# A spectral block with gated MLP: in stage two, the first gate's product two rounds later, the special column's copies behind the W products, three pairs turned first, the first position zero-padded

## The chip, the cores and the metric

One Trainium2 chip, one of its cores. The metric is the device time of one execution in microseconds, the median of three runs; a profiled execution of the same program gives the rows below.

## What is computed

Two branches on x of 2048 x 512 (float32), each gated by rows that come from a condition vector c:

```python
mod = (_silu(c) @ w_mod).reshape(c.shape[0], 6, 1, -1)
sa, ca, ga, sb, cb, gb = (mod[:, 0], ..., mod[:, 5])
h = _layernorm(x, axis=-1) * (1 + ca) + sa
x = x + ga * _A_ref(h, A_w_r, A_w_i)      # irfft2(rfft2(h) * W), W = w_r + i w_i
h = _layernorm(x, axis=-1) * (1 + cb) + sb
x = x + gb * _B_ref(h, B_w1, B_b1, B_w2)  # dense, Mish, dense
```

## The kernel before

The kernel runs in four stages. Stage one makes the row transform and most of the column transform of the normalised x, in 16 steps. Stage two (about 50 to 98 us) finishes the column transform, multiplies by W and begins the transform back. Stage three (`p3_col`, `p3_row`) finishes the transform back and adds the result, gated, to x. Stage four is the MLP.

Stage two treats the 64 column groups as eight **pairs** p of eight groups each, one pair in a round. A pair passes through five helpers:

- `p2_in(p)`: 16 small transposes on TensorE (L469) into two PSUM banks, then two copies back to `a_sb` by ScalarE (L475; for p = 0 one of them by VectorE, L473). The first bank stays in use, since `p2_shift` reads it.
- `p2_shift(p)`: adds a shift to one position; for p of 2 and more VectorE reads the first bank of `p2_in(p)` for it (L487).
- `p2_mul(p)`: eight matmuls (L494) into a bank of tag A, then one of tag B.
- `p2_prod(p)`: the product with W. VectorE reads bank A (L505, L506), then bank B (L507, L509); GpSimd makes a difference (L508) and a sum (L510; for p = 0, 6 and 7 the sum is on VectorE).
- `p2_out(p)`: 32 matmuls (L521) into two banks of tag C, which ScalarE then copies to `dd` in eight instructions (`store_d`, L395 and L396, in the order first bank, second bank, first, second).

PSUM has four tags, A to D, of two banks each. A bank that is to be filled waits until every reader of the tile that held it is done. Two readers of one bank on different engines are put in program order one behind the other.

A round (the loop at L588) issues, in this order: `p2_mul(p)`; `p2_in(p + 2)`; `p2_prod(p)`; `p2_shift(p + 2)`; a share of the sums for the other modulation rows (`mod_late`: VectorE at L554 to L560, ScalarE at L544, GpSimd at L546, from DMAs of `mod_fetch`); `p2_out(p - 1)`. The order is written out by hand (`manual_schedule`): each engine takes its instructions in just this order, and one that waits holds all that follow on its engine. Pairs 0 and 1 are turned (`p2_in`) ahead of the loop.

The special column (group 0 holds two real columns in one) takes a way of its own: `z_in` in round 0 (its copies: `turned`), `z_mul` in round 1, `z_prod` in round 2, `z_back` in round 4, `z_out` behind the loop. `z_back` transposes twice into a bank of tag D (L446, L447) and then makes `t1` and `t2` from it: `turned(t1, ...)` is a copy by ScalarE (L405), a reversed one by VectorE (L406) and a memset by GpSimd (L407); `t2` gets a memset (L450) and three copies on ScalarE, VectorE, ScalarE (L451 to L453). `reflected` (in `z_mul` and `z_out`) multiplies with these; its second matmul (L411) uses a single column of `t` as weights and writes row 0 alone.

`mod_gate` makes the first gate's row over all partitions: a matmul into a bank of tag D (L564), a copy by ScalarE (L566), and on GpSimd the product into `kiv` (L567), which stage three reads at L707. It stands right behind `z_back` in round 4. `apply_gate` does the like for the second gate at the end of the stage (L571, the same matmul form).

Of the kernel before, what the change touches and what calls it, by code (L numbers as in the profile page):

```python
# [12 lines left out]
P = 128  # L13
# [18 lines left out]
def tile_spectral_block(ctx: ExitStack, tc: tile.TileContext, x_d, w1_d, b1_d, w2_d,  # L32
                        c_d, xt_d, wm_d, wq_d, wz_d, kr_d, km_d, kc_d, ki_d, kf_d, kv_d, kw_d, kp_d, out_d):
    nc = tc.nc
# [33 lines left out]
    def bank(tag):  # L68
        return psum.tile([P, 512], F32, name="bank", tag=tag)

    def buf(tag, dt=F32):
        return work.tile([P, 512], dt, name="buf", tag=tag)
# [96 lines left out]
    st = {}  # L169
# [122 lines left out]
    def shift_sums(lo, hi):  # L292
        ps, pick = st["own"]
        own = modr[:, 2].rearrange("p (e q) -> p e q", e=8)
        nc.vector.tensor_tensor(own[:, :, lo:hi], ps.rearrange("p (e q) -> p e q", e=8)[:, :, lo:hi],
                                pick.unsqueeze(2).to_broadcast([P, 8, hi - lo]), op=ALU.mult)
        nc.vector.tensor_reduce(saz[:, lo:hi], own[:, :, lo:hi].rearrange("p e q -> p q e"),
                                axis=mybir.AxisListType.X, op=ALU.add)
# [105 lines left out]
    def turned(dst, src):  # L404
        nc.scalar.copy(dst[:, 0:P], src)  # L405
        nc.vector.tensor_copy(dst[:, P + 1:2 * P], src[:, P - 1:0:-1])  # L406
        nc.gpsimd.memset(dst[:, P:P + 1], 0.0)  # L407

    def reflected(out, t, w, more=()):
        nc.tensor.matmul(out, t[:, 0:P], w(0), start=True, stop=False)  # L410
        nc.tensor.matmul(out[0:1], t[:, 0:1], w(2), start=False, stop=False)  # L411
        for a, b in more:
            nc.tensor.matmul(out, a, b, start=False, stop=False)
        nc.tensor.matmul(out, t[:, P:2 * P], w(1), start=False, stop=True)

    def z_in():
        z = buf("h")
        turned(z, zs[:, 0])
        st["z", 0] = z

    def z_mul():
        z = st.pop(("z", 0))
        pb = bank("D")
        reflected(pb[:, 0:160], z, lambda i: kf[:, 128 + 160 * i:288 + 160 * i])
        st["pb", 0] = pb

    def z_prod():
        pb = st.pop(("pb", 0))
        pbv = pb[:, 0:160].rearrange("p (c j k) -> p c j k", c=2, j=5)
        pr = []  # L430
        for i in range(2):
            t = buf(("g1", "g2")[i])
            tv = t[:, 0:160].rearrange("p (c j k) -> p c j k", c=2, j=5)
            nc.vector.tensor_tensor(tv, pbv, wz[:, i].unsqueeze(1).to_broadcast([P, 2, 5, N2]), op=ALU.mult)
            pr.append(t)
        y = buf("h")
        nc.gpsimd.tensor_tensor(y[:, 0:80], pr[0][:, 0:80], pr[1][:, 80:160], op=ALU.subtract)
        nc.gpsimd.tensor_tensor(y[:, 80:160], pr[0][:, 80:160], pr[1][:, 0:80], op=ALU.add)
        nc.gpsimd.tensor_copy(y[:, 160:256].rearrange("p (i k) -> p i k", i=3),
                              y[:, P:P + 32].unsqueeze(1).to_broadcast([P, 3, 32]))  # L440
        st["y", 0] = y

    def z_back():
        y = st.pop(("y", 0))
        pc = bank("D")
        nc.tensor.transpose(pc[:, 0:P], y[:, 0:P], ident)  # L446
        nc.tensor.transpose(pc[0:96, P:2 * P], y[:, 160:256], ident)  # L447
        t1, t2 = buf("h"), buf("h")
        turned(t1, pc[:, 0:P])
        nc.gpsimd.memset(t2[0:96, 0:P], 0.0)  # L450
        nc.scalar.copy(t2[0:32, 0:P], pc[0:32, P:2 * P])  # L451
        nc.vector.tensor_copy(t2[32:64, 1:P], pc[32:64, 2 * P - 1:P:-1])
        nc.scalar.copy(t2[64:96, 0:1], pc[64:96, P:P + 1])  # L453
        st["t", 0] = t1, t2
# [7 lines left out]

    def p2_in(p):
        tall = zs[:, 8 * p:8 * p + 8].rearrange("p q (i s) -> p i q s", i=2)
        ps = [bank(tag) for tag in ("CC" if p == 1 else "AB")]
        for q in range(8):
            for i in range(2):
                rs = slice(lanes * i, lanes * i + lanes)
                nc.tensor.transpose(ps[i][:, lanes * q:lanes * q + lanes], zs[rs, 8 * p + q], ident[rs, rs])  # L469
        for i in range(2):  # L470
            t = ps[i].rearrange("p (q s) -> p q s", q=8)
            if p == 0 and i == 1:
                nc.vector.tensor_copy(tall[:, i], t)  # L473
            else:
                nc.scalar.copy(tall[:, i], t)  # L475
        st["pt", p] = ps[0]
# [4 lines left out]
    def p2_shift(p):  # L481
        zc = zs[:, 8 * p:8 * p + 8, 0]
        ps = st.pop(("pt", p))[:, 0:8 * lanes:lanes]
        if p < 2:
            nc.gpsimd.tensor_tensor(zc, zc, saz[:, 8 * p:8 * p + 8], op=ALU.add)
        else:
            nc.vector.tensor_tensor(zc, ps, saz[:, 8 * p:8 * p + 8], op=ALU.add)  # L487

    def p2_mul(p):
        st["pb", p] = pbs = []  # L490
        for c in range(2):
            pb = bank("AB"[c])
            for h in range(2):
                nc.tensor.matmul(pb[lanes * h:lanes * h + lanes], kf[:, lanes * c:lanes * c + lanes], z_of(p, h),  # L494
                                 start=True, stop=True)
            pbs.append(pb)

    def p2_prod(p):
        re, im = st.pop(("pb", p))
        wr, wi = ((wqa, wqb)[p // 4][:, p % 4, i] for i in range(2))  # L500
        t = [buf(tag) for tag in ("y", "t", "g1", "g2")]
        st["y", p] = t[:2]
        both = p in (0, pairs - 2, pairs - 1)
        part = bank("A" if p else "D") if both else t[1]
        nc.vector.tensor_tensor(t[0], re, wr, op=ALU.mult)  # L505
        nc.vector.tensor_tensor(part, re, wi, op=ALU.mult)  # L506
        nc.vector.tensor_tensor(t[2], im, wi, op=ALU.mult)  # L507
        nc.gpsimd.tensor_tensor(t[0], t[0], t[2], op=ALU.subtract)  # L508
        nc.vector.tensor_tensor(t[3], im, wr, op=ALU.mult)  # L509
        (nc.vector if both else nc.gpsimd).tensor_tensor(t[1], part, t[3], op=ALU.add)  # L510
# [17 lines left out]
    pairs = NQ // 8  # L528
# [4 lines left out]
    def mod_fetch(which, k):  # L533
        if which < 2:
            w = early[which][:, k]
        else:
            w = hring.tile([P, 512], F32, name="wm", tag="ht", bufs=4)
        late[which, k] = w
        nc.sync.dma_start(w, wm_d[2 + which, k])
# [22 lines left out]
    def mod_gate():  # L562
        ga = bank("D")
        nc.tensor.matmul(ga, ones, modr[:, 0], start=True, stop=True)  # L564
        g = hring.tile([P, 512], F32, name="wm", tag="ht", bufs=4)
        nc.scalar.copy(g, ga)  # L566
        nc.gpsimd.tensor_tensor(kiv, kiv, g.rearrange("p (b a) -> p b a", b=4), op=ALU.mult)  # L567
# [8 lines left out]
    with tc.manual_schedule():  # L576
        for k in range(4):
            mod_fetch(0, k)
        for i in range(4):
            nc.sync.dma_start(wqb[:, i], wq_d[4 + i])  # L580
            mod_fetch(1, i)
        for i in range(4):
            mod_fetch(3 if i % 2 == 0 else 2, i // 2)
        for p in range(2):
            p2_in(p)
            p2_shift(p)
        shift_sums(16, NQ)
        for p in range(pairs):  # L588
            p2_mul(p)
            if p == 0:  # L590
                z_in()
            if p == 0:
                p2_in(2)
            if 1 <= p and p + 2 < pairs:
                p2_in(p + 2)
            p2_prod(p)
            if p == 2:
                z_prod()
            if p + 2 < pairs:
                p2_shift(p + 2)  # L600
            for which, k in work_mod[p]:
                mod_late(which, k)
            if 2 <= p < 6:
                mod_late(3, p - 2)
            if p == 3:
                mod_fetch(3, 2)
            if p == 4:
                mod_fetch(3, 3)
            if p == 5:
                mod_fetch(2, 2)  # L610
                mod_fetch(2, 3)
            if p:
                p2_out(p - 1)
            if p == 1:
                z_mul()
            if p == 4:
                z_back()
                mod_gate()
            if p == 6:
                plus_one(cols[:, 1, 1, :], cols[:, 1, 1, :])  # L620
            if p in (3, 5):
                i = p // 2 - 1
                kc.append(big.tile([P, N2, P], F32, name=f"kc{i}", tag=("cr", "ci")[i]))
                nc.sync.dma_start(kc[i], kc_d[:, i, :, :])
        z_out()
        p2_out(pairs - 1)
        apply_gate()
# [511 lines left out]
```

## Time and profile before

| what | value |
|---|---|
| median of three runs | 390.27 us (389.37 to 390.70) |
| profiled execution, its own time | 388.75 us |
| its span, first to last instruction | 387.0 us |
| TensorE busy | 375.7 us (97%) |
| VectorE busy | 297.9 us (77%) |
| ScalarE busy | 240.1 us (62%) |
| GpSimd busy | 90.9 us (23%) |
| mean granted TensorE clock | 0.991 |

The span is counted from the first to the last instruction; the execution's own time is 1.75 us longer. A clock of 1.00 in a row is the upper of TensorE's two levels (2.4 GHz), 0.50 the lower (1.2 GHz). Times in rows are microseconds from the start of the span.

### The profile page before, as it was taken

The numbers are of one execution on the slowest core, as the hardware profiler recorded it, in microseconds if no ns is written. First come the engines' busy times: TensorE is split into PE (matmuls) and PEld (weight loads), VectorE is DVE, ScalarE is ACT, GpSimd is POOL, SyncE is SP. The second block draws the span as 40 slices with busy tenths as digits, with TensorE's granted clock in tenths as the row PEclk, the third lists the DMA queues.
The fourth block names the chain that finished last, engine by engine and source line by source line (L and its number), as shares of the span: only waits on it lengthen the run. The fifth ranks groups of instructions, "written<-read, shape, count | busy, mean of one in ns | idle before, by whom it ended". The sixth has DMA issues, their size and how long they took to land.

```text
span 387.0 us, 7433 instructions
## 1 busy us (share of the span) xinstructions
PE 375.7 (97%) x2809; PEld 333.6 (86%) x2809; DVE 297.9 (77%) x672; ACT 240.1 (62%) x530; POOL 90.9 (23%) x107
## 2 busy tenths in 40 slices
PE   8999999699998999999999999999999999999996
PEld 7899856447998998998998998999999999899984
DVE  2898988656499999897866965965966875987993
ACT  1788746744449647975755764674674675584750
POOL 0677625752067453210000000000000010017000
PEclk9999999979999999999999999999999999999999
DMA  7999997324132421100100100100100200113011
GB/s 240 382 324 340 354 397 251 116 77 142 57 125 76 129 68 28 56 0 3 54 2 1 56 0 2 54 2 0 58 0 2 75 2 0 55 65 101 3 54 54
DMA packets 20163, 36.78 MB, mean 95 GB/s; under 512 B 3712, under 2 KB 6624, under 8 KB 19872
## 3 DMA queue, kind: packets, MB, share of 16 engines
q1 hardware_dynamic: 20128, 36.31, 27.5%
q8 instruction: 22, 0.36, 0.4%
q14 instruction: 13, 0.11, 0.1%
HBM read 32.10 MB, written 4.20 MB: 94 GB/s over the span
## 4 chain that ended last, share of the span: by engine, by line
PE 80%; DVE 8%; ACT 3%; issue 3%; DMA 3%; POOL 2%; SPq 1%; POOLq 0%; ACTq 0%; DVEq 0%
PE bank L839 24%; PE bank L786 20%; PE bank L788 10%; PE bank L494 4%; PE bank L521 3%; PE bank L213 3%; PE bank L258 3%; PE bank L831 2%; PE bank L851 2%; DVE st L127 2%; PE bank L676 2%; DMA buf<-in_B_w_dram 1%; DMA kr<-in_kr_dram 1%; PE bank L259 1%; DVE x L710 1%
## 5 line engine op out<-in xcount | busy, mean ns | idle before, releaser
L796 ACT ACTIVATE buf<-bank,b1n 128x256 f32<-128x256 f32 (+1 forms) x88 | 40.8, 472 | 64.4 <-PE bank L788 63.4
L797 DVE TENSOR_TENSOR buf<-buf,bank 128x256 f32<-128x256 f32 (+1 forms) x88 | 35.2, 416 | 36.5 <-ACT buf L796 36.5
L749 DVE TENSOR_TENSOR al<-buf,ah 128x512 fp32r<-128x512 f32 (+2 forms) x85 | 53.4, 652 | 0.7 <-ACT ah L748 0.7
L786 PE MATMUL bank<-h2e,w1h 128*128 128x512 f32 (+1 forms) x176 | 47.9, 394 | 0.0
L786 PE MATMUL bank<-h2o,w1h 128*128 128x512 f32 (+1 forms) x176 | 47.8, 393 | 0.0
L768 POOL TENSOR_TENSOR buf<-buf,modr 128x512 f32<-128x512 f32 (+1 forms) x3 | 3.9, 1296 | 180.5 <-DVE buf L797 144.5
L748 ACT CAST ah<-buf 128x512 fp32r<-128x512 f32 (+2 forms) x85 | 43.0, 548 | 1.2 <-DVE buf L813 1.1
L813 DVE TENSOR_TENSOR buf<-buf 128x128 f32<-128x128 f32 x148 | 39.8, 310 | 3.5 <-ACT buf L803 2.2
L803 ACT ACTIVATE buf<-buf 128x512 f32<-128x512 f32 (+1 forms) x48 | 28.6, 596 | 15.0 <-DVE buf L797 14.9
L839 PE MATMUL bank<-w2a,ah 128*128 128x256 f32 x161 | 34.6, 284 | 0.0
L786 PEld LDWEIGHTS bank<-h2e,w1h 128*128 128x128 f32 (+1 forms) x176 | 29.9, 186 | 4.3
L786 PEld LDWEIGHTS bank<-h2o,w1h 128*128 128x128 f32 (+1 forms) x176 | 29.8, 186 | 4.4
L839 PE MATMUL bank<-w2b,ah 128*128 128x256 f32 x147 | 31.3, 279 | 0.0
L788 PEld LDWEIGHTS bank<-h2o,w1l 128*128 128x128 f32 (+1 forms) x176 | 26.8, 185 | 4.0
L788 PEld LDWEIGHTS bank<-h2e,w1l 128*128 128x128 f32 (+1 forms) x176 | 26.7, 186 | 4.0
L788 PE MATMUL bank<-h2e,w1l 128*128 128x256 f32 (+1 forms) x176 | 27.8, 280 | 0.0
L788 PE MATMUL bank<-h2o,w1l 128*128 128x256 f32 (+1 forms) x176 | 27.8, 279 | 0.0
L839 PEld LDWEIGHTS bank<-w2a,ah 128*128 128x128 f32 x161 | 26.3, 188 | 0.0
L698 PE MATMUL bank<-kc,d 128*128 128x128 f32 x128 | 24.8, 275 | 0.0
L697 PE MATMUL bank<-kc,d 128*128 128x128 f32 x128 | 24.7, 275 | 0.0
L839 PEld LDWEIGHTS bank<-w2b,ah 128*128 128x128 f32 x147 | 24.2, 188 | 0.0
L127 DVE BATCH_NORM_STATS2 st<-x 128x6 f32<-128x512 f32 x32 | 22.0, 688 | 0.4
(233 smaller groups left out, 951.3 us busy)
## 6 DMA issues: line engine op xcount, KB each, us to landing
buf<-in_B_w_dram SPq DMA_DIRECT2D x20, 256.0 KB, 2.7
x<-in_A_x_dram SPq DMA_DIRECT2D x16, 256.0 KB, 4.8
xring<-in_x_t_dram SPq DMA_DIRECT2D x16, 256.0 KB, 4.9
out_dram<-x SPq DMA_DIRECT2D x7, 512.0 KB, 2.6
mraw<-in_km_dram SPq DMA_DIRECT2D x16, 128.0 KB, 4.7
wqa<-in_w_q_dram SPq DMA_DIRECT2D x4, 512.0 KB, 6.1
early<-in_w_mod_dram SPq DMA_DIRECT2D x8, 256.0 KB, 6.5
wqb<-in_w_q_dram SPq DMA_DIRECT2D x4, 512.0 KB, 7.2
```

The source lines that it names most:

```text
L127: nc.vector.bn_stats(t, x[:, n, :])
L697: nc.tensor.matmul(o, dj[:, 0:128], kc[0][:, n, :], start=True, stop=False)
L698: nc.tensor.matmul(o, dj[:, 64:192], kc[1][:, n, :], start=False, stop=True)
L748: nc.scalar.copy(h, r)
L749: nc.vector.tensor_tensor(l, r, plain(h), op=ALU.subtract)
L786: nc.tensor.matmul(ps, w1h[:, k, fs], h[:, k], start=(k == 0), stop=False)
L788: nc.tensor.matmul(ps[:, 0:256], w1l[:, k, fs], h[:, k, 0], start=False, stop=(k == 3))
L796: nc.scalar.activation(o, ps[:, 256:], AF.Identity, bias=b1n[:rows, f:f + 1])
L797: nc.vector.tensor_tensor(o, o, ps[:, 0:256], op=ALU.add)
L803: nc.scalar.activation(o, o, AF.Mish)
L813: nc.vector.tensor_tensor(o, p, q, op=op)
L839: nc.tensor.matmul(o, a[p][:, e], w2[t][q][:, r], start=(own and half == 0 and t == 1 and i == 0), stop=(end and i == 2 and (n, half) != ( ...
```

## The change

Five edits, all in stage two.

1. `turned` gets a third block of 128 columns: a memset of it on GpSimd and a copy of the first column into it by ScalarE. The second matmul of `reflected` takes this zero-padded block as weights and writes all rows.
2. `z_back` keeps its two transposes in round 4; the copies that follow them become `z_turn`, called in round 5 behind `p2_prod(5)`.
3. `mod_gate` moves from round 4 (behind `z_back`) to round 6 (behind `p2_out(5)`).
4. Pair 2 is turned ahead of the loop too, and round p turns pair p + 3 instead of p + 2. `p2_shift` stays where it was.
5. Pair 3 is turned into banks of tag C, as pair 1 already was.

```diff
@@ -405,10 +405,12 @@
         nc.scalar.copy(dst[:, 0:P], src)
         nc.vector.tensor_copy(dst[:, P + 1:2 * P], src[:, P - 1:0:-1])
         nc.gpsimd.memset(dst[:, P:P + 1], 0.0)
+        nc.gpsimd.memset(dst[:, 2 * P:3 * P], 0.0)
+        nc.scalar.copy(dst[:, 2 * P:2 * P + 1], src[:, 0:1])
 
     def reflected(out, t, w, more=()):
         nc.tensor.matmul(out, t[:, 0:P], w(0), start=True, stop=False)
-        nc.tensor.matmul(out[0:1], t[:, 0:1], w(2), start=False, stop=False)
+        nc.tensor.matmul(out, t[:, 2 * P:3 * P], w(2), start=False, stop=False)
...
@@ -445,6 +447,10 @@
         pc = bank("D")
         nc.tensor.transpose(pc[:, 0:P], y[:, 0:P], ident)
         nc.tensor.transpose(pc[0:96, P:2 * P], y[:, 160:256], ident)
+        st["pc", 0] = pc
+
+    def z_turn():
+        pc = st.pop(("pc", 0))
         t1, t2 = buf("h"), buf("h")
         turned(t1, pc[:, 0:P])
         nc.gpsimd.memset(t2[0:96, 0:P], 0.0)
@@ -462,7 +468,7 @@
-        ps = [bank(tag) for tag in ("CC" if p == 1 else "AB")]
+        ps = [bank(tag) for tag in ("CC" if p in (1, 3) else "AB")]
@@ -585,17 +591,18 @@
             p2_in(p)
             p2_shift(p)
         shift_sums(16, NQ)
+        p2_in(2)
         for p in range(pairs):
             p2_mul(p)
             if p == 0:
                 z_in()
-            if p == 0:
-                p2_in(2)
-            if 1 <= p and p + 2 < pairs:
-                p2_in(p + 2)
+            if p + 3 < pairs:
+                p2_in(p + 3)
             p2_prod(p)
             if p == 2:
                 z_prod()
+            if p == 5:
+                z_turn()
             if p + 2 < pairs:
                 p2_shift(p + 2)
             for which, k in work_mod[p]:
@@ -615,8 +622,8 @@
                 z_mul()
             if p == 4:
                 z_back()
+            if p == 6:
                 mod_gate()
-            if p == 6:
                 plus_one(cols[:, 1, 1, :], cols[:, 1, 1, :])
```

## Rows read from the trace of the kernel before

**Rows 1.** Waits in 56 to 102 us: us in total, times, longest

```profile
PE bank L564 <- ACT buf L453: 3.1, 1, 3.1
```

**Rows 2.** Windows, TensorE alone: stretch, length, busy (count), clock, DMA share, GB/s

```profile
73.50:74.00 0.50, 0.00 (x1) 1.00 0.08 12
...
76.00:76.50 0.50, 0.00 (x0) 0.50 0.00 0
...
82.50:83.00 0.50, 0.50 (x18) 0.72 0.47 176
...
51.00:52.00 1.00, 0.60 (x4) 1.00 1.07 395
```

**Rows 3.** Chain of waits in order of time: start, us, what

```profile
56.95 1.84 PE bank L521 x28
58.78 0.47 PE bank L410 x2
59.25 0.36 PE bank L411 x2
...
60.09 1.87 PE bank L494 x8
...
66.30 0.66 PE bank L469 x16
...
76.56 2.08 PE bank L564 x2
78.64 3.61 PE bank L494 x8
82.25 0.87 PE bank L469 x12
...
96.87 1.05 PE bank L571 x2
97.92 0.22 PE bank L697 x2
```

**Rows 4.** Timeline of VectorE: start, us, what, idle before it

```profile
58.18 0.16 DVE L487 TENSOR_TENSOR a_sb<-bank,saz 128x8 f32<-128x8 f32 x1
...
61.20 0.69 DVE L505 TENSOR_TENSOR buf<-bank,wqa 128x512 f32<-128x512 f32 x1 [1.41 <-PE bank L494]
61.81 0.68 DVE L506 TENSOR_TENSOR buf<-bank,wqa 128x512 f32<-128x512 f32 x1
...
66.78 0.68 DVE L507 TENSOR_TENSOR buf<-bank,wqa 128x512 f32<-128x512 f32 x1
...
75.25 0.29 DVE L406 COPY buf<-bank 128x127 f32<-128x127 f32 x1 [1.64 <-ACT buf L405]
```

**Rows 5.** Timeline of GpSimd

```profile
68.76 1.29 POOL L510 TENSOR_TENSOR buf<-buf 128x512 f32<-128x512 f32 x1
...
74.27 1.27 POOL L546 TENSOR_TENSOR modr<-modr,wm 128x512 f32<-128x512 f32 x1
...
75.51 0.21 POOL L450 MEMSET buf<- 96x128 f32 x1
```

**Rows 6.** Timeline of ScalarE

```profile
68.47 0.73 ACT L544 ACTIVATE wm<-wm,sc 128x512 f32<-128x512 f32 x1
...
73.17 0.37 ACT L395 COPY d<-bank 128x256 f32<-128x256 f32 x1
...
74.28 0.33 ACT L396 ACTIVATE d<-bank 128x128 f32<-128x128 f32 x1
...
74.70 0.36 ACT L396 ACTIVATE d<-bank 128x128 f32<-128x128 f32 x1
...
75.75 0.26 ACT L451 COPY buf<-bank 32x128 f32<-32x128 f32 x1 [0.53 <-POOL buf L450]
```

**Rows 7.** Lines L410 and L411: weight loads, ns min/median/max

```profile
L410 PEld LDWEIGHTS bank<-kf,buf x2: 186/188/189, 58.7 to 58.8; 128*128 128x128 f32 x2
...
L411 PEld LDWEIGHTS bank<-kf,buf x2: 79/80/82, 59.2 to 59.2; 128*1 128x1 f32 x2
```

## The prediction

> **What bounds the kernel now.** I read the list of waits first. In stage two it has one wait of TensorE that is not a matter of issue: the gate's product (L564) stands 3.1 us behind the last copy of the special column (L453) [rows 1]. The windows come next, and the reader should see two things there. TensorE is idle from 73.5 us, and while it is, its granted clock falls from 1.00 to 0.50; it comes back only at about 82.7 [rows 2]. The chain of waits, read last, gives the price. Idle: from 73.50 to the start of L564 at 76.56, 3.06 us. Clock: L564 takes 2.08 us where the same form takes 1.05 (L571); eight L494 take 3.61 where they take 1.87; sixteen L469 take 0.87 where they take 0.66 [rows 3]. That is 1.03 + 1.74 + 0.21 = 2.98 us. So 6.04 us lie open. Outside this place TensorE works without a gap of note, and stage three begins at 97.92 [rows 3]. Its end moves with that start, so I work out when L697 starts in the changed kernel.
>
> **The change part by part, up to the special column.** Up to here the change buys nothing and adds two kinds of wait, both from banks.
>
> First `p2_out(0)`. Pair 3 now sits in the C banks from round 0, and its first bank is read by `p2_shift(3)` (L487), which stays in round 1 behind `p2_prod(1)`. `p2_out(0)` needs both C banks. VectorE ends that L487 at 58.18 + 0.16 = 58.34 [rows 4], and I see nothing that would bring it earlier, since VectorE's order up to there is the same. `p2_out(0)` began at 56.95 [rows 3]; it now ends some 1.4 us later, as a few matmuls into the free bank go ahead. What turning pair 2 early gains at the start is lost here.
>
> Second, pairs 5, 6 and 7. In round p the bank A of `p2_in(p + 3)` must come from two tiles: `p2_mul(p)`, still to be read by `p2_prod(p)`, or pair p + 2, whose shift stands later in the same round. The earlier is the end of L506. From the start of `p2_mul` (60.09) to that end (61.81 + 0.68 = 62.49) it is 2.40 us [rows 3, 4]; TensorE is through with the eight matmuls after 1.87 [rows 3]. So it waits 0.55 us (with some 0.02 for the handover) in each of rounds 2, 3 and 4: 1.65. `p2_in(4)` in round 1 does not wait, since pair 3 is in C. Below zero neither wait can go: before, these transposes waited for nothing.
>
> The padded block: its weight load is of 128 columns where it was of one, and its matmul takes 0.47 us as its neighbour L410 does, not 0.36 [rows 3]: 0.11 in `z_mul`, 0.11 in `z_out`. Its memset and its copy hide in round 0. The weight loads differ by 188 - 80 = 108 ns [rows 7], four loads in all. The Trainium skill (TensorE: Matmul & The Clock Gate, section LDWEIGHTS) has load time go with the columns alone, columns over 1.2 in ns, that is about nothing for one column. The trace's 80 ns for one column disagrees, its difference of 108 ns agrees; by the page, with all four loads on the path, the padding would cost an estimated 0.4 us in place of 0.22.
>
> So `p2_mul(5)` would start at T = 73.50 + 1.4 + 0.11 + 1.65 = 76.7, with `z_back`'s transposes in front and nothing behind them, where it began at 78.64 [rows 3]. Here the change is 1.9 us ahead, and the clock is up.
>
> **The special column's copies in round 5.** Now the moved copies, by queue. On VectorE L406 and the copy of L452 stand behind L509(5), on GpSimd the memsets stand behind L508(5) and L510(5), on ScalarE the four copies (a new one among them) stand ahead of L544 and of the eight stores of `p2_out(4)`. They alternate, each waiting for the one before, because they share a bank or a tile: L406 waited for L405, L451 for GpSimd's memset [rows 4, 6]. From T:
>
> - L505 starts at T + 1.11 (60.09 to 61.20), L507 two steps of 0.61 later, T + 2.33 [rows 3, 4].
> - From L507's start to L510's end it is 70.05 - 66.78 = 3.27 [rows 4, 5]: T + 5.60.
> - The memsets L407 and L450 ended 0.18 behind GpSimd's previous work (75.54 to 75.72) [rows 5]; a third, of the size of L450, adds 0.2 (bounds 0.1 and 0.3): T + 6.0.
> - From L451's start to L564, which waited for the last copy, it was 76.56 - 75.75 = 0.81 [rows 3, 6]: T + 6.8. The new copy finds room ahead of this.
> - L544 takes up to 0.73 [rows 6]: T + 7.5.
> - The stores open the first C bank after 74.61 - 73.17 = 1.44, the second after 75.06 - 73.17 = 1.89 [rows 6]: T + 9.4.
>
> `p2_out(5)` needs these two banks. TensorE, with `p2_mul(5)`, `p2_out(4)` and `p2_mul(6)` done (1.87 + 1.84 + 1.87 [rows 3]), stands there at T + 5.6. So it waits for 3.8 us, broken by a pair of matmuls into the first bank, that is 3.7. What was queued behind `z_back` on TensorE is now queued on ScalarE: the stall is not gone, it has moved from L564 to L521, one round and a half later. VectorE is held too (L452 at about T + 6.2), but `p2_prod(6)` isn't needed before TensorE resumes.
>
> **The gate.** L564 and L566 in round 6 cost TensorE the same 1.05 us; `kiv` is ready some 8 us before L707 reads it, so this is hidden.
>
> **The sum.** Before, from `p2_mul(5)`'s start to L697: 97.92 - 78.64 = 19.28. Off: the slow clock's 1.74 + 0.21, pair 7's transposes 0.66 (now earlier). On: L564 1.05, padding 0.11, the wait 3.7. That is 21.5, so L697 at 76.7 + 21.5 = 98.2, later than before by 0.3 us, with the clock up throughout.
>
> **The clock.** The trace shows one stall of this kind: 3.06 us idle, clock down before it was over, 2.98 us lost. The new one is longer (3.7), so I expect the same, between 0 and 2.98. I take 2.4, nearer that row, a little under it since the fall may come later in a broken idle. The early waits are short; in 51 to 52 us TensorE was busy for only 0.60 of 1.00 and kept its clock [rows 2].
>
> Sum: +0.3 + 2.4 = +2.7 us on the profiled execution (388.75 becomes 391.4). The median of the runs is 390.27, 1.5 above it, so 393.0.
>
> **The rivals.**
>
> - Forecast, 0.57: stall of `p2_out(5)` with a fall of the clock, 391.5 to 393.6.
> - The clock stays up, 0.15: +0.3, 390.6. For it: idle time is broken by two matmuls. Against: it is longer than the one that let the clock fall.
> - ScalarE isn't held, 0.13: the mechanism is that GpSimd's memsets run early, so that the copies chain up right behind L405 and the stores of `p2_out(4)` come in time. Each microsecond by which the memsets come earlier than T + 6.0 takes one off the stall; at 3.7 it is gone, and with it the fall of the clock: +0.3 - 3.7 = -3.4, 386.9. Against it: GpSimd stood behind L546 in just this way before L450 [rows 5].
> - Besides that the bank waits of rounds 1 to 4 don't arise, 0.06: another -3.05, 383.8. For it: the place of a tile is not seen in the trace.
> - The clock falls in round 1 as well, 0.09: 1.4 us idle beside 0.66 of transposes; another 2.4, 395.4.
>
> Range for 8 in 10: 386.8 to 394.2, from the third case to the forecast's upper end with the memset's bounds; the forecast's own range is 391.5 to 393.6. About 0.3% (1.2 us) is what a measurement of this kernel tells from no change: faster 0.20 (cases three and four), slower 0.62 (forecast, last case, less some of the forecast's low end), same 0.18.
>
> **What would show it.** Right: in the list of waits L521 behind ScalarE's L396 with 3 us or more in one wait, at about 82 to 86 us; ScalarE idle behind GpSimd's memsets just before; L469 idle some 0.5 us behind L506 in three rounds, `p2_out(0)` behind L487; clock 0.50 at about 85 to 92 us. Wrong: no wait of TensorE above 1 us between 76 and 92 us, L697 at 92 to 95.

## The result, and the profile after

The changed kernel takes 390.9 us (median of 20 runs, 389.58 to 391.83) where the kernel before takes 389.36 (20 runs, 387.57 to 391.37): a ratio of 1.0038, with an interval of 1.002 to 1.0055, that is 0.8 to 2.1 us slower. The forecast was slower by 2.7 us, at 393.0, with 391.5 to 393.6 for that case and 386.8 to 394.2 in all. The time lies inside the wide range but below the forecast case's own, and by its number alone it is nearest to the rival in which the clock stays up (390.6). The traces show that the sign and the mechanism are as forecast, the fall of the clock among them; the size is not. The three runs that the forecast started from had a median of 390.27, 0.9 us above that of 20 runs: of the 2.1 us by which the time was missed, this is 0.9, and the change itself was put 1.2 us too high.

In the changed kernel's line numbers `p2_in` is L475 (copies L481), `p2_mul` L500, `p2_prod` L511 to L516, `p2_out` L527, `p2_shift` L493, `z_turn`'s copies L405, L406, L409 and L457 to L459, its memsets L407, L408 and L456, the gate's matmul L570, the second gate's L577, the first matmul of stage three L704.

The list of waits of the changed kernel, 48 to 103 us (us in total, times, longest), answers [rows 1]:

```profile
ACT buf L409 <- POOL buf L408: 4.1, 1, 4.1
...
PE bank L527 <- POOL modr L552: 3.3, 1, 3.3
...
PE bank L475 <- DVE buf L512: 1.9, 3, 0.7
...
PE bank L527 <- DVE a_sb L493: 1.3, 1, 1.3
```

L564's wait behind the special column is gone. In its place stand three kinds of wait that were not there: a long one of `p2_out`, three of the transposes for L512, one of `p2_out(0)` for the shift of pair 3. The timeline of TensorE shows where:

```profile
49.10 1.05 PE L284 MATMUL bank<-kr,cols 128*128 128x128 f32 x8
...
58.79 1.61 PE L527 MATMUL bank<-kv,buf 64*128 64x128 f32 x24 [1.25 <-DVE a_sb L493]
...
63.96 0.71 PE L475 MATMUL bank<-ident,a_sb 64*128 64x64 f32 x16 [0.68 <-DVE buf L512]
...
76.89 1.94 PE L500 MATMUL bank<-a_sb,kf 128*64 128x512 f32 x8
...
85.97 4.08 PE L527 MATMUL bank<-kv,buf 64*128 64x128 f32 x32 [3.28 <-POOL modr L552]
...
99.87 0.38 PE L704 MATMUL bank<-kc,d 128*128 128x128 f32 x2
```

`p2_mul(5)` begins at 76.89 (forecast 76.7, before 78.64 [rows 3]), so here the change is ahead. Then `p2_out(5)` waits 3.28 us. The list names L552 as what ended last before it, but L552 writes `modr`, which `p2_out` doesn't read. The timelines of ScalarE and of GpSimd show the real chain:

```profile
78.31 0.35 ACT L405 COPY buf<-bank 128x128 f32<-128x128 f32 x1
82.76 0.16 ACT L409 COPY buf<-bank 128x1 f32<-128x1 f32 x1 [4.10 <-POOL buf L408]
...
84.42 0.37 ACT L395 COPY d<-bank 128x256 f32<-128x256 f32 x1
...
85.53 0.33 ACT L396 ACTIVATE d<-bank 128x128 f32<-128x128 f32 x1
...
85.95 0.36 ACT L396 ACTIVATE d<-bank 128x128 f32<-128x128 f32 x1
```

```profile
81.27 1.28 POOL L516 TENSOR_TENSOR buf<-buf 128x512 f32<-128x512 f32 x1
...
82.51 0.21 POOL L408 MEMSET buf<- 128x128 f32 x1
...
84.54 1.27 POOL L552 TENSOR_TENSOR modr<-modr,wm 128x512 f32<-128x512 f32 x1 [1.68 <-ACT wm L550]
```

ScalarE stands 4.10 us at L409 for a memset, which stands on GpSimd behind the sum for pair 5 (L516, to 82.55). Behind L409 on ScalarE stand the eight stores of `p2_out(4)`; the first C bank is read out at 85.53 + 0.33 = 85.86, and L527 begins at 85.97. The windows, TensorE alone, answer [rows 2] (stretch, length, busy, clock, DMA share, GB/s):

```profile
85.00:85.50 0.50, 0.00 (x0) 1.00 0.48 45
...
86.00:86.50 0.50, 0.50 (x4) 1.00 1.29 500
86.50:87.00 0.50, 0.50 (x6) 0.50 1.04 344
...
90.00:90.50 0.50, 0.50 (x2) 1.00 0.39 143
```

The clock falls to the lower level, here only when TensorE already works again, and it is back at 90. The 32 matmuls take 4.08 us in this time, where at the upper level they take 2.45 (after_filled_14, below).

### The profile page after: what moved, and what is told of

Same layout as the page of the kernel before. It is cut to its first block, busy times and chain, and to the rows that moved or that the text cites. A ratio compares the mean times of both kernels' runs of the same rounds, so it can differ in the third digit from the quotient of the medians.

```text
span 388.4 us, 7430 instructions
## 1 busy us (share of the span) xinstructions
PE 374.8 (97%) x2809; PEld 335.2 (86%) x2809; DVE 296.4 (76%) x672; ACT 240.1 (62%) x532; POOL 90.9 (23%) x109
## 4 chain that ended last, share of the span: by engine, by line
PE 76%; DMA 8%; DVE 7%; ACT 3%; issue 2%; SPq 2%; POOL 1%; DVEq 0%; POOLq 0%
PE bank L846 23%; PE bank L793 20%; PE bank L795 10%; PE bank L527 3%; PE bank L714 3%; DMA xring<-in_x_t_dram 3%; PE bank L705 3%; PE bank L704 3%; PE bank L838 2%; DMA mraw<-in_km_dram 2%; PE bank L858 2%; DMA modr<-scb 2%; PE bank L683 2%; DMA x<-in_A_x_dram 1%; PE bank L500 1%
## 5 line engine op out<-in xcount | busy, mean ns | idle before, releaser
L756 DVE TENSOR_TENSOR al<-buf,ah 128x512 fp32r<-128x512 f32 (+2 forms) x85 | 53.7, 656 | 0.7 <-ACT ah L755 0.7
L704 PE MATMUL bank<-kc,d 128*128 128x128 f32 x128 | 24.7, 275 | 0.0
L527 PEld LDWEIGHTS bank<-kv,buf 64*128 64x128 f32 x252 | 17.2, 203 | 8.1 <-POOL modr L552 4.9
```

Of the source, the lines that this page charges most:

```text
L527: nc.tensor.matmul(pd[h][:, o], y[c][rs, o], kv[rs, c * P:c * P + P], start=(c == 0), stop=(c == 1))
L704: nc.tensor.matmul(o, dj[:, 0:128], kc[0][:, n, :], start=True, stop=False)
L756: nc.vector.tensor_tensor(l, r, plain(h), op=ALU.subtract)
```

## The experiments

To compare kernels without the start of an execution (in the table's profiles stage one ends up to 1.8 us later in one than in another), I read the **length of stage two** from each profile's timeline of TensorE: from L284 to the first matmul of stage three.

| kernel | median us | its ratio to the kernel before on the same chip | L284, first of stage three | length |
|---|---|---|---|---|
| before | 389.36 | 1 | 48.70, 97.76 | 49.06 |
| changed | 390.9 | 1.0038 (1.002 to 1.0055) | 49.10, 99.87 | 50.77 |
| turning_only | 389.94 | 1.0031 (1.0003 to 1.0058) | 48.88, 97.70 | 48.82 |
| old_turning | 386.9 | 0.9958 (0.9935 to 0.998) | 49.67, 95.45 | 45.78 |
| stores_first | 386.92 | 0.995 (0.9931 to 0.997) | 50.20, 96.54 | 46.34 |
| gate_only | 384.96 | 0.9903 (0.9871 to 0.9934) | 49.86, 93.70 | 43.84 |
| pad_only | 388.75 | 1.0008 (0.9982 to 1.0035) | 48.99, 94.97 | 45.98 |
| before_filled_13 | 387.01 | 0.9926 (0.9901 to 0.9951) | 50.02, 96.15 | 46.13 |
| after_filled_14 | 388.95 | 0.9984 (0.9959 to 1.0008) | 49.38, 98.51 | 49.13 |
| after_again | 390.95 | 1.0043 (1.0012 to 1.0073) | 49.73, 100.47 | 50.74 |
| both_undone | 384.29 | 0.9893 (0.986 to 0.9926) | 50.46, 93.44 | 42.98 |
| gate_in_7 | 383.71 | 0.984 (0.9814 to 0.9866) | 50.12, 93.12 | 43.00 |

**Theory and rival.** The theory is the prediction's: early waits for banks, and the stall of L564 moved to `p2_out(5)` through ScalarE's queue. The rivals are that the early waits are made up later, that `p2_out(5)` waits for GpSimd (as the list of waits says), and that the slow matmuls have another cause than the idle time.

### The gate alone

```diff
--- before
             if p == 4:
                 z_back()
-                mod_gate()
             if p == 6:
+                mod_gate()
                 plus_one(cols[:, 1, 1, :], cols[:, 1, 1, :])
```

> The kernel before with one edit: mod_gate moves from round 4 to round 6; the special column's copies stay in z_back. If TensorE's stall of 3.06 us and the fall of its clock (2.98 us) hang on L564 alone waiting for the bank that the last copy L453 reads, TensorE goes straight from z_back's transposes to p2_mul(5); VectorE's copies still hold L505(5) until 76.3, so GpSimd's sum for pair 5 ends near 80.8 and p2_out(5) waits about 1 us for it. That is 5 us less than before: 384.4 (383.4 to 385.5), clock at 1.00 through the stage. The rival, that ScalarE and VectorE held by the copies stall the next C or A bank just as long: 388 to 389.5, with a wait of 2 us or more in round 5 or 6.

Measured: 384.96 us, ratio 0.9903; the length of stage two falls from 49.06 to 43.84. One moved line takes the stall and the fall of the clock away; the granted clock of the execution is 1.000. The new wait is there with the 1 us I gave it: `p2_out(5)` puts four matmuls ahead of it, stands idle for 0.35 us before the others, and takes 83.81 - 80.82 = 2.99 us up to the next instruction, where `p2_out(4)` takes 1.94.

```profile
74.60 1.94 PE L494 MATMUL bank<-a_sb,kf 128*64 128x512 f32 x8
...
80.82 0.87 PE L521 MATMUL bank<-kv,buf 64*128 64x128 f32 x4
82.05 1.83 PE L521 MATMUL bank<-kv,buf 64*128 64x128 f32 x28 [0.35 <-POOL buf L510]
83.81 1.12 PE L564 MATMUL bank<-modr,ones 128*128 128x512 f32 x2
```

So of the five edits this one holds the gain, and the others must have cost more than it brings.

### Stores ahead of the copies

```diff
--- after
-            if p == 5:
-                z_turn()
             if p + 2 < pairs:
                 p2_shift(p + 2)
...
             if p:
                 p2_out(p - 1)
+            if p == 5:
+                z_turn()
```

> The changed kernel with z_turn called behind p2_out(4) in round 5 instead of behind p2_prod(5): ScalarE's stores of p2_out(4) now stand ahead of the special column's copies. If the 3.28 us stall of p2_out(5) comes from these stores queued behind the copies, it goes, and the clock stays up: 3.3 + 2.1 = 5.4 us less than the changed kernel, 385.5 (384.5 to 386.5). What stays is the early waits (1.25 in round 1, 0.6 to 0.7 in each of rounds 2 to 4). The rival, that p2_out(5) waits for GpSimd (L552, which the list of waits names): the order on GpSimd gives L552 no later, the stall shrinks by less than 1 us: 389.5 to 391.

Measured: 386.92 us, ratio 0.995, a little above the expected 384.5 to 386.5. The stall of `p2_out(5)` is gone (it begins at 83.72, right behind `p2_mul(6)`), the clock is at 1.000, the stage 4.4 us shorter than the changed kernel's. GpSimd's order around L552 isn't what held it. 1 us of the expected 5.4 is missing in the profile (by the ratios of the runs 2 us): VectorE is late behind the copies, and the last `p2_out` now waits for pair 7's difference:

```profile
83.72 2.23 PE L527 MATMUL bank<-kv,buf 64*128 64x128 f32 x32
...
93.52 2.12 PE L527 MATMUL bank<-kv,buf 64*128 64x128 f32 x32 [1.17 <-POOL buf L514]
```

### The turning order, taken out and alone

```diff
--- after (old_turning); turning_only is the reverse of this, on the kernel before
-        ps = [bank(tag) for tag in ("CC" if p in (1, 3) else "AB")]
+        ps = [bank(tag) for tag in ("CC" if p == 1 else "AB")]
...
-        p2_in(2)
         for p in range(pairs):
...
-            if p + 3 < pairs:
-                p2_in(p + 3)
+            if p + 2 < pairs:
+                p2_in(p + 2)
```

> The changed kernel with the order of p2_in of before (pair 2 in round 0, pair p + 2 in round p, only pair 1 in C banks); z_turn, mod_gate and the padding stay changed. If the bank waits of rounds 1 to 4 cost 3.2 us of TensorE, less what turning pair 2 ahead of the loop gains at the start (0.5 to 0.8), TensorE is 2.4 us earlier at p2_mul(5); the stall of p2_out(5) stays at about 3 us, with its fall of the clock: 388.5 (387.5 to 389.5). The rival, that these waits are made up later: 390.5 to 391.

> The kernel before with only the turning order changed (pair 2 ahead of the loop, pair p + 3 in round p, pairs 1 and 3 in C banks). If the bank waits of rounds 1 to 4 are the cost of this edit, it is 2.4 us slower than before: 391.8 (390.8 to 392.8), with waits of L469 for L506 of 0.5 to 0.7 us in three rounds, one of L521 for L487 of some 1.3 us, and z_back's stall as before. The rival, that turning early pays for itself: 388.5 to 389.5.

Measured: old_turning 386.9 us, ratio 0.9958, which is 0.8% or 3.1 us below the changed kernel's 1.0038; I had expected 2.4. turning_only 389.94 us, ratio 1.0031, 1.2 us slower by the ratio; I had expected 2.4. Both medians lie below the expected ranges. turning_only has the early waits and `z_back`'s stall, old_turning the stall of `p2_out(5)` alone, as expected. Timeline of TensorE of turning_only, then of old_turning:

```profile
64.02 0.71 PE L469 MATMUL bank<-ident,a_sb 64*128 64x64 f32 x16 [0.68 <-DVE buf L506]
...
79.93 1.12 PE L564 MATMUL bank<-modr,ones 128*128 128x512 f32 x2 [2.90 <-ACT buf L453]
80.99 1.94 PE L494 MATMUL bank<-a_sb,kf 128*64 128x512 f32 x8
```

```profile
83.18 2.45 PE L527 MATMUL bank<-kv,buf 64*128 64x128 f32 x32 [2.78 <-POOL modr L552]
```

In neither profile did the clock fall behind the stall: L564 takes 1.12 and the eight L494 1.94 after 2.90 us of idle time, L527 2.45 after 2.78. So the price of the clock isn't fixed. The twelve runs of turning_only make this plain (time, mean granted clock of the execution):

```
388.65 0.998   388.66 0.998   388.75 0.998   388.90 0.999   388.99 0.999   389.01 0.999
390.88 0.996   391.01 0.995   391.55 0.995   391.90 0.995   392.27 0.991   392.40 0.994
```

Six at some 388.8 with the clock nearly whole, six at some 391.7 with it lower, about 2.9 apart. Half of the executions lose about what the profile of the kernel before lost, half lose next to nothing. The early waits themselves are confirmed: without a fall of the clock the stage takes 48.82 against 46.13 (before_filled_13), 2.7 us more.

### The padding alone

```diff
--- before
         nc.gpsimd.memset(dst[:, P:P + 1], 0.0)
+        nc.gpsimd.memset(dst[:, 2 * P:3 * P], 0.0)
+        nc.scalar.copy(dst[:, 2 * P:2 * P + 1], src[:, 0:1])
...
-        nc.tensor.matmul(out[0:1], t[:, 0:1], w(2), start=False, stop=False)
+        nc.tensor.matmul(out, t[:, 2 * P:3 * P], w(2), start=False, stop=False)
```

> The kernel before with the zero-padded block alone (a memset and a copy more in each of the two turned calls, the second matmul of reflected with 128 columns of weights). The copies in z_back get a memset and a copy longer, in the middle of the stall of L564: about 0.2 to 0.4 us more there, and 0.11 in each of z_mul and z_out: 389.9 (389.4 to 390.4). The rival, that the matmul with one row out was the slow one: 388.8 to 389.3.

Measured: 388.75 us against 388.74 on the same chip, ratio 1.0008: no difference to be seen, and less than the 389.4 to 390.4 expected. In the profile the stall is 3.19 in place of 3.06, but `z_mul` is shorter: from L412 to the next round's L496 it is 60.02 - 59.01 = 1.01 us, where the kernel before takes 60.09 - 58.78 = 1.31 [rows 3].

```profile
59.01 0.54 PE L412 MATMUL bank<-kf,buf 128*128 128x160 f32 x2
59.38 0.43 PE L413 MATMUL bank<-kf,buf 128*128 128x160 f32 x2
59.65 0.43 PE L416 MATMUL bank<-kf,buf 128*128 128x160 f32 x2
60.02 1.94 PE L496 MATMUL bank<-a_sb,kf 128*64 128x512 f32 x8
...
76.69 1.12 PE L566 MATMUL bank<-modr,ones 128*128 128x512 f32 x2 [3.19 <-ACT buf L455]
77.75 1.94 PE L496 MATMUL bank<-a_sb,kf 128*64 128x512 f32 x8
```

The rival had the sign right: the form with a single column of weights was the slower one, by 0.3 us in `z_mul`, where I had booked the padding as a cost of 0.11. The matmul with the single column isn't longer itself (0.43 us in both profiles); the steps to it, from it and behind its neighbour are each 0.1 us longer. Here too the clock did not fall behind the stall (1.12 and 1.94).

### The idle time filled

```diff
--- before (26 calls, then 13)
                 z_back()
+                warm(26)
                 mod_gate()
--- after (28 calls, then 14)
+            if p == 6:
+                warm(28)
             if p:
                 p2_out(p - 1)
```

`warm` multiplies ones by ones into a spare bank; nothing reads it.

> The changed kernel with 28 matmuls of 128 x 128 (ones by ones, into a spare bank of tag B, results unused) ahead of p2_out(5) on TensorE: they run in the idle time while p2_out(5) waits, some 3.1 us, so they add work and take no wait away. If the slow p2_out(5) (4.08 us for 2.0) comes from the clock falling because TensorE was idle, the clock stays at 1.00 and the time falls by about 2 us: 388.9 (388.2 to 389.7). The rival, that p2_out(5) is slow by its banks: 390.5 to 391.3.

> The kernel before with 26 such matmuls between z_back's transposes and L564, in the 3.06 us of idle time. If that idle time is what lets the clock fall, the clock stays at 1.00, L564 takes 1.05 us and p2_mul(5) 1.87, and the time falls by about 3 us: 386.4 (385.7 to 387.3), with runs that scatter less than the 3.8 us of the kernel before. The rival, that the loss of clock is hidden behind other engines: 389 to 389.7.

Measured: 392.81 and 389.35 us, 1.9 us and 0.6 us slower than without the fill (the first against runs of another chip). The experiment missed its aim: a call takes 0.22 us and not 0.11, so 26 calls ran 5.97 us in an idle time of 3.06 and pushed the rest back. The clock did stay up (0.999 and 1.000). Half as many calls fit:

> The kernel before with 13 matmul calls of ones by ones between z_back's transposes and L564. In the run with 26 calls these ran 5.8 us, so 13 run 2.9 us and fit into the 3.06 us of idle time: no work is pushed back, and only the clock is changed. So the time that this takes off is what the fall of the clock costs before, over many executions and not in the one profile: if the profile (2.98 us lost) is typical, 386.3; if the fall costs less in most executions, as the profile of pad_only (idle 3.19 us, no slow matmul behind it) suggests, about 1.5 us less than before, 387.4 to 387.9.

> The changed kernel with 14 such calls (3.1 us) ahead of p2_out(5), inside the 3.28 us of its wait. What this takes off is what the fall of the clock costs in the changed kernel: by the profile 1.6 to 2.1 us, 389.0 to 389.4; if the price is the same as in the kernel before, both fills take the same off and the clock drops out of the comparison of the two kernels.

> The changed kernel as it is, on the chip of the two fills, so that the price of its clock is read from runs of one chip: 390.5 to 391, 1.2 to 1.8 us over the kernel before.

Measured on one chip: the kernel before 389.33, filled 387.01; the changed kernel 390.95, filled 388.95. Timeline of TensorE of before_filled_13, then of after_filled_14:

```profile
74.66 3.07 PE L303 MATMUL bank<-ones 128*128 128x128 f32 x26
77.89 1.12 PE L564 MATMUL bank<-modr,ones 128*128 128x512 f32 x2 [0.16 <-ACT buf L453]
```

```profile
82.89 3.39 PE L303 MATMUL bank<-ones 128*128 128x128 f32 x28
86.24 2.45 PE L527 MATMUL bank<-kv,buf 64*128 64x128 f32 x32
```

The fills push nothing back: from L284 to L564 it is 27.87 us with the fill and 27.86 without, to the matmuls of `p2_out(5)` 36.86 and 36.87. Work that nobody needs, put into idle time, makes both kernels 2 us faster, and only the clock is different. So the idle time is the cause of the fall, and its price over many executions is 2.32 us before and 2.00 us after. `p2_out(5)` at the full clock still takes 2.45 and not 2.06: it waits inside for the second C bank, some 0.4 us (in the changed kernel's profile ScalarE ends its reading of that bank at 85.95 + 0.36 = 86.31, L527 begins at 85.97).

### Both costs taken out, and the gate later still

`both_undone` is the changed kernel with the turning order of before and `z_turn` behind `p2_out(4)`; `gate_in_7` moves `mod_gate` in it behind `p2_out(6)` as well:

```diff
--- both_undone
-            if p == 6:
+            if p == 7:
                 mod_gate()
+            if p == 6:
                 plus_one(cols[:, 1, 1, :], cols[:, 1, 1, :])
```

> The changed kernel with both costs taken out: the turning order of before and z_turn behind p2_out(4). What is left is the gate in round 6, the copies in round 5 behind the stores, and the padding. If the early waits and the stall of p2_out(5) are all that the change cost, TensorE has no wait above 0.5 us between 50 and 95 us and a clock of 1.00, and the two prices add: 390.9 - 2.4 - 5.4 = 383.1 (382.3 to 384.2), below both kernels and below the gate alone by about 1 us. The rival, that the copies only move a wait on to p2_out(6) or to VectorE: 385 to 387.

> both_undone (turning order of before, copies behind the stores of p2_out(4)) with mod_gate one round later still, behind p2_out(6) in round 7. In both_undone the last p2_out waits 1.08 us for GpSimd's L514 of pair 7, which is late because VectorE is, not TensorE; L570 (1.05 us) moved from ahead of p2_mul(7) to behind p2_out(6) would lie in that wait: 0.8 us less, 383.5 (383.0 to 384.3). If p2_prod(7) moves up no further with p2_mul(7), it is the same as both_undone, 384.3.

Measured: both_undone 384.29 us (ratio 0.9893), 1.2 above the 383.1 to which the two expected prices added up; gate_in_7 383.71 (ratio 0.984), the fastest here and faster than both kernels. The stage takes 42.98 and 43.00 us, so moving the gate once more brings nothing in stage two: in both VectorE is what is late, and the wait only changes its place. Timeline of TensorE of both_undone, then of gate_in_7:

```profile
90.43 2.12 PE L527 MATMUL bank<-kv,buf 64*128 64x128 f32 x32 [1.08 <-POOL buf L514]
```

```profile
83.85 1.94 PE L500 MATMUL bank<-a_sb,kf 128*64 128x512 f32 x8 [0.84 <-DVE bank L512]
...
90.10 2.12 PE L527 MATMUL bank<-kv,buf 64*128 64x128 f32 x32 [0.33 <-POOL buf L514]
```

What gate_in_7 has over both_undone in its profile lies behind the start of stage three (288.6 us to the end against 289.5), not where I expected it.

## Why the prediction was right in its mechanism and wrong in its size

**Right.** The two bank waits ahead of the special column are there with their sizes: `p2_out(0)` 1.25 (forecast 1.4), three times L475 0.68, 0.63 and 0.62 (forecast 0.55 each). `p2_mul(5)` starts at 76.89 (76.7). The stall of `p2_out(5)` has the place and the cause that the prediction gave, ScalarE held at L409 behind GpSimd's memset; it is 3.28 + 0.4 inside L527 = 3.7 us, the forecast's value. stores_first shows that this queue is the cause: the stall went when the stores went ahead. That `p2_mul(5)` starts so near the forecast is in part luck. Counted from L284, the place where `p2_mul(5)` starts is 2.99 us later than the end of `z_back`'s transposes before, and the sum had 3.16; but `p2_out(0)` ends 1.2 later (forecast 1.4), rounds 2 to 4 are 2.1 longer (forecast 1.65), since a wait holds its round up by more than the idle time shown, and `z_mul` is 0.3 shorter (forecast 0.11 longer). The filled kernels give stage two without the clock: 49.13 - 46.13 = +3.0 us, where the prediction has +0.3 + 2.98 = +3.3.

**Wrong, by the steps of the sum:**

| step | forecast, us | runs, us |
|---|---|---|
| stage two at the full clock, after less before | +3.3 | +3.0 |
| of this the padding | +0.22 | about -0.15 (pad_only 45.98, before_filled_13 46.13: 0.3 off in `z_mul`, 0.13 on in the stall) |
| "its end moves with that start": stage three and four | 0 | -0.6 |
| fall of the clock, after less before | 2.4 - 2.98 = -0.6 | 2.00 - 2.32 = -0.3 |
| sum | +2.7 | +2.1 |
| the runs | | +1.5 (20 runs), +1.6 (after_again) |

The step that failed by most is "Its end moves with that start": whatever lies behind the start of stage three was put at nothing, from a look at stage two alone. From the first matmul of stage three to the end it is 387.0 - 98.51 = 288.5 us in after_filled_14 and 385.2 - 96.15 = 289.05 in before_filled_13; in the two kernels themselves 288.5 and 289.2. The difference is one gap of TensorE in stage three, in the kernel before and in the changed one:

```profile
118.65 1.16 PE L707 MATMUL bank<-kiv,buf 128*128 128x128 f32 x8 [1.08 <-ACT buf L700]
```

```profile
120.10 1.16 PE L714 MATMUL bank<-kiv,buf 128*128 128x128 f32 x8 [0.42 <-ACT buf L707]
```

The gap is 1.07 to 1.09 us in before with its fills, gate_only, both_undone, turning_only, pad_only and stores_first, and 0.35 to 0.42 in the changed kernel with its fills, old_turning and gate_in_7. It isn't set by the start alone, since gate_in_7 starts first of all and has the small gap. The copy that ends it (L700, L707 in the changed kernel) stands on ScalarE behind L132, which waits for VectorE: 1.88 us before, 1.23 in the changed kernel. Of these 0.65 us VectorE loses 0.45 at its two subtractions L749 (L756) some 8 us earlier, the rest in the few operations behind them. Lines from the timelines of VectorE, GpSimd and ScalarE, of before, then of the changed kernel:

```profile
106.79 0.73 POOL L745 TENSOR_TENSOR modr<-buf 128x256 f32<-128x256 f32 x1
106.83 2.10 DVE L749 TENSOR_TENSOR w<-buf,w 128x256 fp32r<-128x256 f32 x2
...
114.72 0.30 ACT L132 ACTIVATE rstd<-mv,eps 128x2 f32<-128x2 f32 x1 [1.88 <-DVE mv L128]
```

```profile
108.94 1.65 DVE L756 TENSOR_TENSOR w<-buf,w 128x256 fp32r<-128x256 f32 x2
109.12 0.92 POOL L752 TENSOR_TENSOR modr<-buf 128x256 f32<-128x256 f32 x1
...
116.17 0.29 ACT L132 ACTIVATE rstd<-mv,eps 128x2 f32<-128x2 f32 x1 [1.23 <-DVE mv L128]
```

All fourteen profiles fall into these two kinds. Where GpSimd's first L745 (L752) begins 0.04 to 0.06 us before VectorE's two subtractions, these take 2.10 us and the gap is large; where VectorE begins first, by 0.13 to 0.19 us, they take 1.59 to 1.65, L745 takes 0.92 in place of 0.73, and the gap is small. No run changed this order alone, so that it sets the gap is read from the profiles and not shown by an experiment. Why GpSimd comes later in one kind stays open: ScalarE's third L700, ahead of it in the chain, begins 6.78 us behind the first matmul of the stage in place of 6.51.

The second is the padding, booked with the wrong sign: +0.22 where the profiles give about -0.15.

The third is the price of the clock, read from one execution. The profile of before lost 2.98 us; over the runs it is 2.32. The forecast took 2.4 for the new stall and it is 2.00. Here the two errors nearly cancel, but the loss isn't a constant: in the 26 runs of before beside the fills, the ten below 388 us have mean clocks of 0.993 to 1.000, the six above 390.7 of 0.989 to 0.991. A change judged against one profile can be off by up to the 2.9 us that separate the two halves of turning_only's runs.

The rest, 0.5 us between +2.1 and the runs, is within the intervals and stays open. It doesn't lie in the clock: the two filled kernels differ by 388.95 - 387.01 = 1.94 us in their medians, where their profiles give 3.0 - 0.6 = 2.4. Of the rivals, ScalarE held or not was settled against the rival (4.10 us at L409), the bank waits came as told, the clock did not fall in round 1 (1.25 us idle there), and "the clock stays up" is true of executions of other kernels here (old_turning's profile, half of turning_only's runs), but hardly of the changed kernel, of whose 20 runs one has a mean clock of 0.998 and the others 0.990 to 0.996.

The prediction found 6.04 us open at L564, and gate_only alone brings 4.2 in the medians. It was also right that the other edits would spend this gain and more.

## What to carry to other kernels

When an operation is moved off the path of one engine, follow it through the queue of every engine that it has instructions on: here copies that no longer held TensorE held ScalarE, and ScalarE's next eight instructions freed the banks that TensorE needed. Look at each instruction of a chain that hops between engines for what stands ahead of it there; the hop through GpSimd behind a 1.28 us sum was the long one. Before several edits are bundled, try the smallest alone: one moved call took 1% off, and the bundle around it gave all of that back and 1.5 us more.

## What the runs showed of the hardware that was not expected

- A matmul whose weights are a single column was not cheaper here than one with 128: with zero-padded weights the three matmuls of `z_mul` take 1.01 us in place of 1.31, and the weight load of 80 ns [rows 7] saved nothing. In the profile of pad_only the weight loads of the second and third begin 0.13 us ahead of their matmuls (59.25 and 59.38, 59.52 and 59.65), in that of before together with them (59.18, 59.55).
- About 3 us of idle time of TensorE let its clock fall from 2.4 to 1.2 GHz in some executions and not in others: the profile of before after 3.06 us and both profiles of the changed kernel after 3.28, the profiles of pad_only (3.19), turning_only (2.90) and old_turning (2.78) not. turning_only's runs split six to six, about 2.9 us apart.
- Matmuls that compute nothing of use, put into the idle time, keep the clock up (mean 0.995 to 1.000 in 21 runs) and take 2.0 to 2.3 us off the median.
- Two operations on VectorE and GpSimd that overlap went with a different length according to which began first: VectorE's two subtractions took 2.10 us when 0.05 us behind GpSimd's, 1.6 when ahead of it, and GpSimd's took 0.73 or 0.92. TensorE's gap some 11 us later differed by 0.7 us.
